# The hidden tile of the first MoE stays in PSUM until its gates

## The chip, the cores and the metric

The kernel runs on one core of a Trainium2 chip. The core has a matrix engine (TensorE, here PE, with its weight loads as PEld), a vector engine (VectorE, DVE), a scalar engine (ScalarE, ACT), a general engine (GpSimd, POOL) and a queue engine (SyncE, SP). Each works through its own list of instructions in order and waits on semaphores for the others. Matmuls write PSUM, eight banks of 128 partitions by 512 fp32 words; everything else lies in SBUF. The metric is the device time of one launch in microseconds. The kernel before took 3349.0 us, the median of three runs (3348.02 to 3355.43).

## The reference

Three stages follow each other: a two-dimensional Fourier transform of 8 x 3072 x 256 numbers of which the real part is kept, a dense MoE layer with 2048 hidden units, and a routed MoE with 8 experts of 1024 hidden units, where each token goes to one expert.

```python
X = np.fft.fft(np.fft.fft(x, axis=1), axis=2).real          # 8 x 3072 x 256
h = X.reshape(-1, 256) @ w_in                               # 24576 x 2048
g = h * np.clip(h + 3.0, 0.0, 6.0) / 6.0
y = g @ w_out                                               # 24576 x 256
logits = y @ w_gate                                         # 8 experts
e = argmax(logits); p = softmax(logits)[e]
out = p * (np.maximum(y @ w1[e], 0.0) @ w2[e])              # by expert
```

## The kernel before, in words

Precision comes from pairs: a number is kept as a rounded high part and the rest as a low part, and a product takes three matmuls (high-high, high-low, low-high).

The first phase runs the Fourier transform and the first MoE. The transform along the 256 columns is folded into `w_in`, which gives the two stacks `WA` and `WB`; the transform along the 3072 rows is done by pieces: folds of the input (`fold_quarter`, `fold_whole`, mostly on VectorE, part on GpSimd), splits into high and low (`stack_splits`), and matmuls against tables (`fft_g0`, `fft_g12`). There are 24 groups (8 batches by 3), each of two chunks of 256 column pairs, that is 512 tokens. A chunk takes 8 steps, one for each 256 hidden units, so that phase one has 384 steps; 48 of them make a batch.

`step(s)` (L943) records one step: `mm1` makes the tile `ab` (14 matmuls of 256 columns into two banks, one for WA and one for WB); `mm2` of the step three back adds its gated tile `gh`, `gl` to the four accumulators `acc` (24 matmuls of 264 columns); then come the vector parts. `h_of` (L493) copies the first bank to `A` on ScalarE (L496), and VectorE writes A minus the second bank and A plus the second bank to the two halves of `h` in SBUF (L184 and L181 are the helpers `sub` and `add`). For the step before, `relu6` (L501, ScalarE) makes `r` from `h`, `gate_h` (L508, VectorE) writes min(r, 1) times h over `r`, ScalarE rounds it to `gh` (L959), and GpSimd writes the rest `gl` (L184). So `r`, `gh` and `gl` of step s carry the number s + 1 in the names before.

PSUM: the pool `ab_ps` has two tiles of two banks, `acc` takes the other four banks. Every piece of the row transform takes a tile of `ab_ps` too (`f`, `fe`, `fo`), and so do the preparations of the weights in the first ten steps (`wi`, `wot`) and a few parts near the end (`exa`, `exo`, `ec`, `rk`). A tile is free when all that read it are done.

Every eighth step (s % 8 = 2) ends a chunk: the accumulators are copied out (`xo`, L532), cut into halves (`xp`, L539, two instructions), the tokens are routed (`rt_...` on VectorE, counts and scattered rows by GpSimd), and one piece of the next transform runs in the same step, six in a batch.

The order on each engine is set by a scheduler that lists instructions by priority and by a forecast of when their inputs are ready; `keep_in_program_order` pins an instruction to the order in which it was recorded. In the kernel before it pins the folds on VectorE (`pinned`), not the matmuls. The second phase, the routed MoE (from about 2150 us on), is not touched.

Of the kernel before, what the change touches and what calls it, by code (L numbers as in the profile page):

```python
# [10 lines left out]
F32 = mybir.dt.float32  # L11
# [5 lines left out]
AF = mybir.ActivationFunctionType  # L17
# [9 lines left out]
GW = 264  # L27
# [16 lines left out]
EC = 5  # L44
EX = 6
RKW = 4
BUFS = dict(h=2, r=4, gh=4, gl=4)
EXTRA = 23
LATE = (0, 0, 1, 1, 2, 3, 3, 4, 5, 5, 6, 6, 7, 7, 8, 8, 8, 9)
RK = 2  # L50
# [24 lines left out]
def tile_fft_moe(ctx, tc, xr, xf, xcoef, w_in, w_out, w_gate, w1, w2, tabs, fm, misc, tri, sgn8, dstc, maskc, out):  # L75
# [24 lines left out]
    tiles, hold = {}, {}  # L100
# [21 lines left out]
    def wo(i, f):  # L122
        if (i, f // 8) not in WOh:
            WOh[i, f // 8] = pc.tile([P, 8, GW], F32R, tag=f"WO{i}{f // 8}", name=f"WO{i}{f // 8}")
        return WOh[i, f // 8][:, f % 8]
# [20 lines left out]
    dve, act, pool, pe, sp = nc.vector, nc.scalar, nc.gpsimd, nc.tensor, nc.sync  # L146
# [6 lines left out]
    def ab_tile(name):  # L153
        hold["last"] = t = ab_ps.tile([P, 2, 512], F32, tag="ab", name=name)
        return t


    def bank(name):
        if "hp" in hold:
            return hold["hp"].tile([P, 512], F32, tag="hp", name=name)  # L160
        return ab_tile(name)[:, 1]

    def mm_group(dst, terms):
        for n, (l, r) in enumerate(terms):
            pe.matmul(dst, l, r, start=(n == 0), stop=(n == len(terms) - 1))  # L165

    def pinned(i):
        if hold.get("fold"):
# [11 lines left out]
    def add(eng, o, a, b):  # L180
        pinned(eng.tensor_tensor(out=o, in0=a, in1=b, op=ALU.add))  # L181

    def sub(eng, o, a, b):
        i = eng.tensor_tensor(out=o, in0=a, in1=b, op=ALU.subtract)  # L184
        pinned(i)
        return i
# [82 lines left out]
    def fft_g0(b, pq):  # L269
        def e_mm(st):  # L270
            ab = st["ab"] = ab_tile(f"fe{b}_0")
            mm_group(ab[:, 0, 0:258], fft_terms(SC0, 0, 0, "c", 0) + xterm(b, X_T0, 258))
            mm_group(ab[:, 1, 0:256], fft_terms(SC0, 1, 0, "c", 1))

        def e_ev(st):
            ab = st["ab"]
            v = lambda i: pq[:, i].rearrange("p (a c) -> p a c", a=2)
            act.activation(v(0), ab[:, :, 0:256], AF.Copy)
            dve.tensor_copy(pex[:, b:b + 1], ab[:, 0, 256:257])
            dve.tensor_tensor(out=v(1), in0=ab[:, :, 0:256], in1=v(0), op=ALU.subtract)  # L280

        def o_mm(st):
            ab = st["ab2"] = ab_tile(f"fo{b}_0")
            for i, n, c0 in ((0, 258, X_T0 + P), (1, 256, X_T1)):
                full = fft_terms(SS0, 1 - i, 0, "s", i) + xterm(b, c0, n)
                edge = fft_terms(SC0, i, P, "c", i, 1)
                for t, (l, r) in enumerate(full[:1] + edge + full[1:]):
                    rows = slice(0, 1 if 0 < t <= len(edge) else P)
                    pe.matmul(ab[rows, i, 0:n], l, r, start=t == 0, stop=t == len(full + edge) - 1)

        def o_ev(st):
            ab = st["ab2"]
            v = lambda i: pq[:, i].rearrange("p (a c) -> p a c", a=2)
            act.activation(v(2), ab[:, :, 0:256], AF.Copy)
            dve.tensor_copy(qex[:, b:b + 1], ab[:, 0, 256:257])
            dve.tensor_tensor(out=v(3), in0=ab[:, :, 0:256], in1=v(2), op=ALU.subtract)

        return [(e_mm, e_ev), (o_mm, o_ev)]
# [191 lines left out]
        for i in range(2):  # L490
            mm_group(ab[:, 1, i * 256:(i + 1) * 256], [(WB[a][:, f[i]], pq[:, 2 + c, c0:c0 + 256]) for a, c in PASS])

    def h_of(ab, h, s):  # L493
        A = pw.tile([P, 2, 256], F32, tag="Ac", bufs=AB, name=f"A{s}")
        v = [ab[:, n].rearrange("p (i n) -> p i n", i=2) for n in range(2)]
        act.activation(A, v[0], AF.Copy)  # L496
        sub(dve, h[0], A, v[1])
        add(dve, h[1], A, v[1])

    def relu6(r, h):  # L500
        act.activation(r, h, AF.Relu, bias=half, scale=1.0 / 6.0)  # L501


    def halves(tag, dt, s):
        return [pw.tile([P, 2, 256], dt, tag=tag, bufs=BUFS[tag], name=f"{tag}{s}_{n}") for n in range(2)]

    def gate_h(g, r, h):
        dve.scalar_tensor_tensor(out=g, in0=r, scalar=1.0, in1=h, op0=ALU.min, op1=ALU.mult)  # L508

    def mm2(acc, gh, gl, f0, first, last, mid=(), ntau=4):  # L510
        def one(i, t, g, w, st, sp_):
            lhs = g[t // 2][:, i, (t % 2) * P:(t % 2 + 1) * P]
            pe.matmul(acc[t][:, 0:GW], lhs, wo(w, f0 + i), start=st, stop=sp_)  # L513
        for i in range(2):
            for t in range(ntau):
                one(i, t, gh, 0, first and i == 0, False)
                one(i, t, gh, 1, False, False)
            if i == 0:
                for f in mid:
                    f()  # L520
        if last:
            for t in range(ntau):
                for i in range(2):
                    one(i, t, gl, 0, False, i == 1)
        else:
            for i in range(2):
                for t in range(ntau):
                    one(i, t, gl, 0, False, False)
# [78 lines left out]
    if True:  # L607
# [52 lines left out]
        NS = len(chunks) * STEPS  # L660
# [257 lines left out]
        def plan_early():  # L918
            e0 = 8 * (NCH - EC) + 18 + RKW - 3
            fill[e0].append(lambda: None)  # L920
            pfill[e0].append(early_mm)
            fill[e0].append(early_pick)
            fill[e0 + 4].append(lambda: (first_sets(), load_x(0), load_w(0), load_x(1)))
            for n in range(4):
                fill[e0 + 6 + EG * n].append(lambda n=n: in_order(prep_w(0, lambda n: dve)[n]))
            fill[e0 + 10 + EX].append(lambda: prep_x(0))

        def step(s):
            z = s - LAG
            if s < NS:  # L930
                b, g, c = chunks[s // STEPS]
                f0 = 2 * (s % STEPS)
                ab = ab_tile(f"ab{s}")
                mm1(ab, f0, gt[(b, g)], c * 256, q3[s // STEPS % 2])
            hold["ride"] = None
            for f in pfill.pop(s, []):
                f()
            hold["ride"] = None
            if 0 <= z < NS:
                k = z % STEPS  # L940
                if k == 0:
                    hold["acc"] = [ac_ps.tile([P, 512], F32, tag=f"acc{t}", name=f"acc{z}_{t}") for t in range(4)]
                mm2(hold["acc"], *hold.pop(("g", z)), 2 * k, k == 0, k == STEPS - 1, mfill.pop(s, []))  # L943
            for f in afill.pop(s, []):
                f()
            hold["ride"] = None
            if s < NS:
                h = hold["h", s] = halves("h", F32, s)
                h_of(ab, h, s)
            if 0 < s <= NS:  # L950
                h = hold.pop(("h", s - 1))
                r, gh, gl = halves("r", F32, s), halves("gh", F32R, s), halves("gl", F32R, s)
                g = r
                for n in range(2):
                    relu6(r[n], h[n])
                for n in range(2):
                    gate_h(g[n], r[n], h[n])
                for n in range(2):
                    act.activation(gh[n], g[n], AF.Copy)  # L959
                for n in range(2):  # L960
                    sub(pool, gl[n], g[n], gh[n])
                hold[("g", s - 1)] = (gh, gl)
            if 0 <= z < NS and z % STEPS == STEPS - 1:
                xo = pw.tile([P, 4, GW], F32, tag="xo", bufs=1, name=f"xo{z}")
                xp = pw.tile([P, 4, XW], I32, tag="xp", name=f"xp{z}")
                with tc.high_priority(offset=6):
                    evac(hold["acc"], xo)
                halve(xo, xp)
                ci = z // STEPS
                b, g, c = chunks[ci]  # L970
                plan_routing(routing(xo, xp, ci * 4, 4, 0 if (g == 0 and c == 0) else None, f"c{ci}",
                             RKW if ci < NCH - 2 else 3), s + 1)
            for f in fill.pop(s, []):
                f()
            if s % STEPS == QB and s + STEPS < NS:
                load_q3(s // STEPS + 1)

        x0 = (NB - 1) * 6 * STEPS + EXTRA
        fill[x0 - 1].append(lambda: plan_extra(x0))
        plan_early()  # L980
        for s in range(NS + LAG):
            step(s)
        ps1.close()
        h_ps = ctx.enter_context(tc.tile_pool(name="h_ps", bufs=4, space=PSUM, reuse_waits="tile"))
        o_ps = ctx.enter_context(tc.tile_pool(name="o_ps", bufs=4, space=PSUM, reuse_waits="tile"))
# [33 lines left out]
        ge = pw.tile([P, NTILE, NE + 1], F32, tag="xp", name="ge")  # L1019
        tt = pw.tile([P, NTILE, NE], F32, tag="r", bufs=BUFS["r"], name="tt")  # L1020
        dve.memset(ge[:, :, 0:1], 1.0)
# [94 lines left out]
        full = last  # L1116
# [3 lines left out]
        n = nc.values_load(nus[0:1, 0:1], min_val=0, max_val=NSMALL, skip_runtime_bounds_check_because=why)  # L1120
# [159 lines left out]
```

## Time and profile before

| | |
|---|---|
| median of three runs | 3349.0 us |
| the profiled execution | 3351.21 us, span 3349.4 us |
| mean granted TensorE clock | 0.979 |
| PE busy | 3133.1 us (94%) |
| PEld busy | 3001.7 us (90%) |
| DVE busy | 2277.1 us (68%) |
| ACT busy | 1934.1 us (58%) |
| POOL busy | 2267.7 us (68%) |

The profile is of one execution. Busy shares are means over the two phases; matmul ends are modelled, so that a busy PE isn't yet PE at its peak. The chain that ended last is 45% PE, 18% DVE, 17% ACT and 9% issue. A wait is put down to what ended it last.

### The profile page before, as it was taken

The numbers are of one execution on the slowest core, as the hardware profiler recorded it, in microseconds if no ns is written. First come the engines' busy times: TensorE is split into PE (matmuls) and PEld (weight loads), VectorE is DVE, ScalarE is ACT, GpSimd is POOL, SyncE is SP. The second block draws the span as 40 slices with busy tenths as digits, with TensorE's granted clock in tenths as the row PEclk, the third lists the DMA queues.
The fourth block names the chain that finished last, engine by engine and source line by source line (L and its number), as shares of the span: only waits on it lengthen the run. The fifth ranks groups of instructions, "written<-read, shape, count | busy, mean of one in ns | idle before, by whom it ended". The sixth has DMA issues, their size and how long they took to land.

```text
span 3349.4 us, 62616 instructions
## 1 busy us (share of the span) xinstructions
PE 3133.1 (94%) x23482; PEld 3001.7 (90%) x23482; DVE 2277.1 (68%) x3699; ACT 1934.1 (58%) x3339; POOL 2267.7 (68%) x1784
## 2 busy tenths in 40 slices
PE   5899999999999999999899999999999999999998
PEld 5899999899899899899899999988888888898887
DVE  8878777777777777777777676755555555555553
ACT  3566666566666566666566666645454444544453
POOL 5567776776776777677777776766676666666664
PEclk8999999999999999999999999999999999999999
DMA  5100100100100110000000002065555555545560
GB/s 180 61 28 21 36 25 14 43 24 16 39 28 16 33 33 16 30 30 17 31 14 16 14 18 51 20 193 154 144 168 149 143 149 158 147 145 154 147 171 30
DMA packets 256195, 243.18 MB, mean 73 GB/s; under 512 B 157739, under 2 KB 219020, under 8 KB 255888
## 3 DMA queue, kind: packets, MB, share of 16 engines
q1 hardware_dynamic: 234640, 184.66, 19.7%
q0 software_dynamic: 21248, 54.48, 4.5%
q8 instruction: 187, 3.06, 0.4%
q14 instruction: 120, 0.98, 0.1%
HBM read 159.71 MB, written 54.04 MB: 64 GB/s over the span
## 4 chain that ended last, share of the span: by engine, by line
PE 45%; DVE 18%; ACT 17%; issue 9%; POOL 5%; SPq 0%; DMA 0%; ACTq 0%; POOLq 0%; DVEq 0%
PE op L165 16%; PE hp L165 15%; PE acc L513 8%; ACT gh L959 7%; ACT r L501 6%; PE ab L165 5%; DVE h L184 4%; POOL gl L184 3%; DVE r L508 2%; POOL xs_dram L149 2%; DVE R L189 2%; DVE R L181 2%; DVE H L181 1%; ACT xp L539 1%; ACT xo L532 1%
## 5 line engine op out<-in xcount | busy, mean ns | idle before, releaser
L184 POOL TENSOR_TENSOR gl<-r,gh 128x512 fp32r<-128x512 f32 x768 | 1109.6, 1464 | 468.1 <-ACT gh L959 372.7
L501 ACT ACTIVATE r<-h,half 128x512 f32<-128x512 f32 x768 | 546.4, 719 | 610.1 <-DVE h L184 386.0
L508 DVE SCALAR_TENSOR_TENSOR r<-r,h 128x512 f32<-128x512 f32 x768 | 625.1, 818 | 369.3 <-ACT r L501 368.2
L513 PE MATMUL acc<-WO,gh 128*128 128x264 f32 x6144 | 824.4, 287 | 3.4 <-ACT xo L532 3.4
L513 PEld LDWEIGHTS acc<-WO,gh 128*128 128x128 f32 x6144 | 786.2, 192 | 3.6 <-ACT xo L532 3.6
L165 PE MATMUL ab<-pq,WA 128*128 128x256 f32 x2304 | 398.8, 290 | 107.4 <-DVE h L181 68.4
L995 DVE SCALAR_TENSOR_TENSOR WB<-hp,WA 128x512 fp32r<-128x512 f32 (+1 forms) x472 | 278.5, 606 | 301.8 <-ACT WA L994 301.7
L959 ACT ACTIVATE gh<-r 128x512 fp32r<-128x512 f32 x768 | 451.1, 622 | 42.6 <-DVE r L508 13.6
L513 PE MATMUL acc<-WO,gl 128*128 128x264 f32 x3072 | 444.6, 286 | 2.7 <-POOL gl L184 1.8
L165 PEld LDWEIGHTS ab<-pq,WA 128*128 128x128 f32 x2304 | 333.6, 193 | 120.3 <-issue 87.3
L513 PEld LDWEIGHTS acc<-WO,gl 128*128 128x128 f32 x3072 | 404.6, 189 | 6.1 <-POOL gl L184 5.6
L994 ACT ACTIVATE WA<-hp 128x512 fp32r<-128x512 f32 (+1 forms) x472 | 240.9, 529 | 197.5 <-PE hp L165 194.3
L165 PE MATMUL ab<-pq,WB 128*128 128x256 f32 x2304 | 349.2, 289 | 0.0
L149 POOL DMA_INDIRECT out_dram<-yo,dst x200 | 217.3, 1086 | 155.9 <-DVE yo L1095 118.3
L165 PEld LDWEIGHTS ab<-pq,WB 128*128 128x128 f32 x2304 | 314.2, 197 | 0.0
L149 POOL DMA_INDIRECT xs_dram<-xp,pic x192 | 212.6, 1107 | 125.6 <-DVE pic L599 68.9
L165 PE MATMUL hp<-xTb,TB 128*128 128x512 f32 (+1 forms) x1344 | 277.8, 364 | 13.9 <-DVE WB L995 13.9
L165 PE MATMUL hp<-xTa,W1b 128*128 128x512 f32 (+1 forms) x1392 | 277.0, 358 | 2.2 <-DVE WB L995 2.2
L165 PEld LDWEIGHTS hp<-xTb,TB 128*128 128x128 f32 x1344 | 226.3, 188 | 58.1 <-DVE WB L995 15.5
L165 PE MATMUL op<-W2b,WA 128*128 128x256 f32 x1536 | 276.3, 282 | 0.0
L165 PEld LDWEIGHTS hp<-xTa,W1b 128*128 128x128 f32 x1392 | 228.8, 189 | 43.3 <-DVE WB L995 2.6
L184 DVE TENSOR_TENSOR h<-A,ab 128x512 f32<-128x512 f32 x384 | 259.4, 675 | 6.7 <-ACT A L496 6.1
(269 smaller groups left out, 5479.7 us busy)
## 6 DMA issues: line engine op xcount, KB each, us to landing
w1a<-in_w_dram SPq DMA_DIRECT2D x29, 1024.0 KB
w1b<-in_w_dram SPq DMA_DIRECT2D x29, 1024.0 KB
w2b<-in_w_dram SPq DMA_DIRECT2D x58, 512.0 KB
R<-in_xr_dram SPq DMA_DIRECT2D x32, 774.0 KB
w2a<-in_w_dram SPq DMA_DIRECT2D x29, 768.0 KB
w2d<-in_w_dram SPq DMA_DIRECT2D x28, 256.0 KB
q<-pq SPq DMA_DIRECT2D x288, 1.0 KB
raw<-in_w_in_dram SPq DMA_DIRECT2D x8, 512.0 KB
```

The costliest lines, as they stand in the source:

```text
L149: i = pool.indirect_dma_start(oob_is_err=False, **kw)
L165: pe.matmul(dst, l, r, start=(n == 0), stop=(n == len(terms) - 1))
L181: pinned(eng.tensor_tensor(out=o, in0=a, in1=b, op=ALU.add))
L184: i = eng.tensor_tensor(out=o, in0=a, in1=b, op=ALU.subtract)
L189: pinned(dve.scalar_tensor_tensor(out=o, in0=a, scalar=s, in1=b, op0=ALU.mult, op1=ALU.add))
L501: act.activation(r, h, AF.Relu, bias=half, scale=1.0 / 6.0)
L508: dve.scalar_tensor_tensor(out=g, in0=r, scalar=1.0, in1=h, op0=ALU.min, op1=ALU.mult)
L513: pe.matmul(acc[t][:, 0:GW], lhs, wo(w, f0 + i), start=st, stop=sp_)
L532: act.activation(xo[:, t, :], acc[t][:, 0:GW], AF.Copy)
L959: act.activation(gh[n], g[n], AF.Copy)
L994: act.activation(hi, ps, AF.Relu)
L995: dve.scalar_tensor_tensor(out=lo, in0=ps, scalar=0.0, in1=hi, op0=ALU.max, op1=ALU.subtract)
```

## The change

`h` has no place in SBUF any more. `h_of` writes the difference and the sum over the two banks of the `ab` tile they were made from, and `relu6` and `gate_h` read them there; a tile of `ab_ps` is free only after both gates. ReLU is recorded in the step that makes h, the gates, the rounding and the rest one step later. While the steps are recorded (`hold["steps"]`), each matmul of the helpers is pinned to the program's order. `gl` has six buffers in place of four, and `h` none.

```diff
-BUFS = dict(h=2, r=4, gh=4, gl=4)
+BUFS = dict(r=4, gh=4, gl=6)
...
+    def matmul(*a, **kw):
+        i = pe.matmul(*a, **kw)
+        if hold.get("steps"):
+            tc.keep_in_program_order(i)
+
     def mm_group(dst, terms):
         for n, (l, r) in enumerate(terms):
-            pe.matmul(dst, l, r, start=(n == 0), stop=(n == len(terms) - 1))
+            matmul(dst, l, r, start=(n == 0), stop=(n == len(terms) - 1))
...
-    def h_of(ab, h, s):
+    def h_of(ab, s):
         A = pw.tile([P, 2, 256], F32, tag="Ac", bufs=AB, name=f"A{s}")
-        v = [ab[:, n].rearrange("p (i n) -> p i n", i=2) for n in range(2)]
-        act.activation(A, v[0], AF.Copy)
-        sub(dve, h[0], A, v[1])
-        add(dve, h[1], A, v[1])
+        h = [ab[:, n].rearrange("p (i n) -> p i n", i=2) for n in range(2)]
+        act.activation(A, h[0], AF.Copy)
+        sub(dve, h[0], A, h[1])
+        add(dve, h[1], A, h[1])
+        return h
...
             if s < NS:
-                h = hold["h", s] = halves("h", F32, s)
-                h_of(ab, h, s)
-            if 0 < s <= NS:
-                h = hold.pop(("h", s - 1))
+                h = h_of(ab, s)
                 r, gh, gl = halves("r", F32, s), halves("gh", F32R, s), halves("gl", F32R, s)
-                g = r
                 for n in range(2):
                     relu6(r[n], h[n])
+                hold["r", s] = h, r, gh, gl
+            if 0 < s <= NS:
+                h, r, gh, gl = hold.pop(("r", s - 1))
                 for n in range(2):
-                    gate_h(g[n], r[n], h[n])
+                    gate_h(r[n], r[n], h[n])
...
+        hold["steps"] = True
         for s in range(NS + LAG):
             step(s)
+        hold["steps"] = False
```

The second matmul loops of `fft_g0` and `mm2` call the same helper. Three places show what the order becomes.

ScalarE at the end of a chunk, step 106, before. `r107` is made from the h of step 106, `xo103` and `xp103` are the chunk's result, `vc2` is the transform's second bank:

```order
L496 ACTIVATE A106_8267<-ab106_8210 128x512
L501 ACTIVATE r107_0_8360<-h106_0_8265,half_101 128x512
L959 ACTIVATE gh106_0_8273<-r106_0_8271 128x512
L532 ACTIVATE xo103_8285<-acc96_0_7759 128x264
L532 ACTIVATE xo103_8285<-acc96_1_7760 128x264
L532 ACTIVATE xo103_8285<-acc96_2_7761 128x264
L959 ACTIVATE gh106_1_8274<-r106_1_8272 128x512
L532 ACTIVATE xo103_8285<-acc96_3_7762 128x264
L501 ACTIVATE r107_1_8361<-h106_1_8266,half_101 128x512
L539 ACTIVATE xp103_8286<-xo103_8285 128x4x256 x2
L321 ACTIVATE vc2_1_1_8293<-f2_1_1_8249 128x258
L496 ACTIVATE A107_8356<-ab107_8311 128x512
```

The same place now (names carry the step's own number):

```order
L502 ACTIVATE A106_8061<-ab106_8006 128x512
L965 ACTIVATE gh105_0_7993<-r105_0_7991 128x512
L965 ACTIVATE gh105_1_7994<-r105_1_7992 128x512
L508 ACTIVATE r106_0_8065<-ab106_8006,half_101 128x512
L508 ACTIVATE r106_1_8066<-ab106_8006,half_101 128x512
L539 ACTIVATE xo103_8079<-acc96_0_7569 128x264
L539 ACTIVATE xo103_8079<-acc96_1_7570 128x264
L539 ACTIVATE xo103_8079<-acc96_2_7571 128x264
L539 ACTIVATE xo103_8079<-acc96_3_7572 128x264
L326 ACTIVATE vc2_1_1_8087<-f2_1_1_8045 128x258
L546 ACTIVATE xp103_8080<-xo103_8079 128x4x256 x2
L182 ACTIVATE pq2_1_7493<-pf2_1_1_8088 128x512
```

The two roundings `gh` stand ahead of the two `r`, and no longer between them, and `vc` stands ahead of `xp`. In a plain step the list is A, r, gh, gh, r before and A, gh, gh, r, r now.

VectorE in plain steps, 109 and the start of 110, before; L189 is a fold of the transform's input:

```order
L184 TENSOR_TENSOR h109_0_8493<-A109_8495,ab109_8454 128x512
L181 TENSOR_TENSOR h109_1_8494<-A109_8495,ab109_8454 128x512
L508 SCALAR_TENSOR_TENSOR r110_0_8574<-r110_0_8574,h109_0_8493 128x512
L508 SCALAR_TENSOR_TENSOR r110_1_8575<-r110_1_8575,h109_1_8494 128x512
L189 SCALAR_TENSOR_TENSOR R3_1_1_8087<-R3_1_1_8087 128x6x129
L184 TENSOR_TENSOR h110_0_8568<-A110_8570,ab110_8529 128x512
```

The same steps now:

```order
L189 TENSOR_TENSOR ab109_8244<-A109_8283,ab109_8244 128x512
L186 TENSOR_TENSOR R3_1_1_7887<-R3_1_1_7887 128x6x129
L186 TENSOR_TENSOR ab109_8244<-A109_8283,ab109_8244 128x512
L515 SCALAR_TENSOR_TENSOR r109_0_8287<-r109_0_8287,ab109_8244 128x512
L515 SCALAR_TENSOR_TENSOR r109_1_8288<-r109_1_8288,ab109_8244 128x512
L189 TENSOR_TENSOR ab110_8317<-A110_8356,ab110_8317 128x512
L194 SCALAR_TENSOR_TENSOR R3_1_1_7887<-R3_1_1_7887 128x6x129
```

The fold moved from behind the gates to between the difference and the sum. The gates of a step stand ahead of the next step's h in both lists, though they are recorded behind it now.

TensorE in the first steps, behind `mm1` of step 3, before; `wot` and `wi` prepare weights:

```order
L513 MATMUL acc0_3_677<-WO10_491,gh1_1_479 128x264
L513 MATMUL acc0_0_674<-WO00_490,gl1_0_480 128x264
L473 MATMUL wot1_634<-ident_95,rawo_148 128x128 x4
L513 MATMUL acc0_1_675<-WO00_490,gl1_0_480 128x264
L513 MATMUL acc0_2_676<-WO00_490,gl1_1_481 128x264
L513 MATMUL acc0_3_677<-WO00_490,gl1_1_481 128x264
L513 MATMUL acc0_0_674<-WO00_490,gl1_0_480 128x264
L513 MATMUL acc0_1_675<-WO00_490,gl1_0_480 128x264
L513 MATMUL acc0_2_676<-WO00_490,gl1_1_481 128x264
L513 MATMUL acc0_3_677<-WO00_490,gl1_1_481 128x264
L165 MATMUL wi5_645<-SC1_74,fmt_140 128x256 x4
L165 MATMUL wot1_634<-wg_158,wotT1_639 128x8 x4
```

The same place now:

```order
L164 MATMUL ab3_621<-pq0_0_213,WB1_72 128x256
L478 MATMUL wot1_636<-ident_95,rawo_148 128x128 x4
L164 MATMUL wot1_636<-wg_158,wotT1_641 128x8 x4
L164 MATMUL wi5_647<-SC1_74,fmt_140 128x256 x12
L164 MATMUL wi5_647<-fmt_140,SC1_74 128x2 x4
L164 MATMUL wi5_647<-SC1_74,fmt_140 128x128 x4
L164 MATMUL wi5_647<-fmt_140,SC1_74 128x2 x4
L164 MATMUL wi5_647<-SC1_74,fmt_140 128x128 x4
L164 MATMUL acc0_0_676<-WO00_494,gh0_0_407 128x264
```

`wot` and `wi` stood in and behind the accumulator's matmuls, and stand ahead of them now, right behind `mm1`. From step 13 to step 361 the matmuls stand in the same order in both.

## Rows read from the trace of the kernel before

**Rows 1.** Busy time by window: us, busy us (count) by engine, clock, DMA share, GB/s.

```profile
868.00:1127.00 259.00, 239.91 (x1925) 235.90 (x1925) 198.44 (x329) 164.53 (x305) 184.96 (x167) 0.98 0.08 26
```

**Rows 2.** TensorE's waits, 1055 to 1314.6 us: total us, times, longest.

```profile
PE ab L165 <- DVE h L181: 10.1, 7, 2.0
...
PE acc L513 <- POOL gl L184: 0.2, 1, 0.2
```

**Rows 3.** Timeline of TensorE: start us, us, instruction, count, idle time before it.

```profile
1013.96 0.86 PE L165 MATMUL f<-TB,SC 128*128 128x256 f32 x6
...
1015.68 0.59 PE L165 MATMUL ab<-pq,WA 128*128 128x256 f32 x3
...
1040.11 0.52 PE L165 MATMUL ab<-pq,WA 128*128 128x256 f32 x3
...
1044.67 0.52 PE L165 MATMUL ab<-pq,WA 128*128 128x256 f32 x3
...
1055.03 0.95 PE L165 MATMUL fe<-TB,SC0s 128*128 128x258 f32 x6 [0.78 <-DVE h L181]
...
1058.89 0.59 PE L165 MATMUL ab<-pq,WA 128*128 128x256 f32 x3 [2.01 <-DVE h L181]
...
1314.60 0.95 PE L165 MATMUL fe<-TB,SC0s 128*128 128x258 f32 x6 [0.78 <-DVE h L181]
```

**Rows 4.** Busy time by window, just behind the wait of 2.01 us.

```profile
1060.00:1063.80 3.80, 3.80 (x21) 3.80 (x21) 2.18 (x5) 3.80 (x8) 2.25 (x3) 0.58 0.01 2
```

**Rows 5.** Timeline of VectorE, two steps with a fold ahead of them.

```profile
1051.91 1.78 DVE L189 SCALAR_TENSOR_TENSOR H<-H 128x516 f32<-128x516 f32 x1
1053.62 0.67 DVE L184 TENSOR_TENSOR h<-A,ab 128x512 f32<-128x512 f32 x1
1054.21 0.68 DVE L181 TENSOR_TENSOR h<-A,ab 128x512 f32<-128x512 f32 x1
...
1056.80 0.75 DVE L508 SCALAR_TENSOR_TENSOR r<-r,h 128x512 f32<-128x512 f32 x1 [0.97 <-ACT r L501]
1057.47 0.67 DVE L184 TENSOR_TENSOR h<-A,ab 128x512 f32<-128x512 f32 x1
```

**Rows 6.** Timeline of ScalarE in the same steps.

```profile
1054.38 0.72 ACT L501 ACTIVATE r<-h,half 128x512 f32<-128x512 f32 x1
...
1056.06 0.71 ACT L501 ACTIVATE r<-h,half 128x512 f32<-128x512 f32 x1
```

**Rows 7.** Groups, 1055 to 1314.6 us: count | busy us, mean ns | idle before.

```profile
L508 DVE SCALAR_TENSOR_TENSOR r<-r,h 128x512 f32<-128x512 f32 x96 | 75.6, 791 | 48.3 <-ACT r L501 48.2
L184 DVE TENSOR_TENSOR h<-A,ab 128x512 f32<-128x512 f32 x48 | 32.4, 675 | 0.0
...
L189 DVE SCALAR_TENSOR_TENSOR R<-R 128x774 f32<-128x774 f32 x4 | 6.0, 1501 | 0.0
...
L181 DVE TENSOR_TENSOR R<-R 128x516 f32<-128x516 f32 x4 | 4.9, 1230 | 0.0
...
L184 POOL TENSOR_TENSOR gl<-r,gh 128x512 fp32r<-128x512 f32 x96 | 137.9, 1456 | 54.2 <-ACT gh L959 46.7 <-PE acc L513 6.4 <-DVE pf L323 0.2
L149 POOL DMA_INDIRECT xs_dram<-xp,pic x24 | 26.7, 1114 | 16.3 <-DVE pic L599 9.9 <-issue 4.6 <-DVE rt_kc L559 0.9
...
L501 ACT ACTIVATE r<-h,half 128x512 f32<-128x512 f32 x97 | 69.1, 719 | 83.7 <-DVE h L184 51.6 <-POOL gl L184 23.4 <-DVE h L181 7.0
```

**Rows 8.** A ReLU out of PSUM in the second phase, group over the span.

```profile
L994 ACT ACTIVATE WA<-hp 128x512 fp32r<-128x512 f32 x328 | 192.9, 593 | 184.0 <-PE hp L165 180.9 <-PE rkc L165 2.3 <-PE cps L1013 0.8
```

**Rows 9.** Timeline at a chunk's end: ScalarE, then TensorE.

```profile
1018.40 2.02 ACT L539 ACTIVATE xp<-xo 128x1024 uint16<-128x1024 uint16 x2
...
1021.71 0.60 PE L165 MATMUL ab<-pq,WA 128*128 128x256 f32 x3 [1.20 <-DVE rt_kc L585]
```

**Rows 10.** Timeline of TensorE, steps 3 and 4.

```profile
80.78 0.95 PE L165 MATMUL ab<-pq,WA 128*128 128x256 f32 x3
...
91.37 0.57 PE L165 MATMUL ab<-pq,WA 128*128 128x256 f32 x3
```

More of the change, by code (lines that the diff above doesn't have):

```diff
@@ L288, in o_mm @@
                     rows = slice(0, 1 if 0 < t <= len(edge) else P)
-                    pe.matmul(ab[rows, i, 0:n], l, r, start=t == 0, stop=t == len(full + edge) - 1)
+                    matmul(ab[rows, i, 0:n], l, r, start=t == 0, stop=t == len(full + edge) - 1)
         def o_ev(st):
@@ L512, in one @@
             lhs = g[t // 2][:, i, (t % 2) * P:(t % 2 + 1) * P]
-            pe.matmul(acc[t][:, 0:GW], lhs, wo(w, f0 + i), start=st, stop=sp_)
+            matmul(acc[t][:, 0:GW], lhs, wo(w, f0 + i), start=st, stop=sp_)
         for i in range(2):
@@ L947, in step @@
             if s < NS:
-                h = hold["h", s] = halves("h", F32, s)
-                h_of(ab, h, s)
-            if 0 < s <= NS:
-                h = hold.pop(("h", s - 1))
+                h = h_of(ab, s)
                 r, gh, gl = halves("r", F32, s), halves("gh", F32R, s), halves("gl", F32R, s)
-                g = r
                 for n in range(2):
                     relu6(r[n], h[n])
+                hold["r", s] = h, r, gh, gl
+            if 0 < s <= NS:
+                h, r, gh, gl = hold.pop(("r", s - 1))
                 for n in range(2):
-                    gate_h(g[n], r[n], h[n])
+                    gate_h(r[n], r[n], h[n])
                 for n in range(2):
-                    act.activation(gh[n], g[n], AF.Copy)
+                    act.activation(gh[n], r[n], AF.Copy)
                 for n in range(2):
-                    sub(pool, gl[n], g[n], gh[n])
-                hold[("g", s - 1)] = (gh, gl)
+                    sub(pool, gl[n], r[n], gh[n])
+                hold["g", s - 1] = gh, gl
             if 0 <= z < NS and z % STEPS == STEPS - 1:
```

## The prediction

> **What bounds the kernel now.** I read the busy time by window first. In one batch of the middle PE is busy 239.9 of 259 us and no other engine more than 198.4 [rows 1], so the time is PE's, and what can be gained is what PE loses. From a `fe` to the same piece one batch later takes 259.57 us, a plain step 4.56, a transform piece 1.72 [rows 3]. 48 plain steps are 218.9; five pieces at 1.72 and the longer `fo` (26 matmuls), which I take at 3.5, add 12.1: 231. So 28.5 us of a batch are lost, 4.75 at each of its six chunk ends.
>
> The waits of PE come next: seven rows, 10.1 us for VectorE's sum `h` in the first, 19.8 in all [rows 2]. They stand at the transform pieces, which take a tile of `ab_ps`: 0.78 ahead of `fe`, 2.01 ahead of the `ab` behind it [rows 3]. Behind the 2.01 the granted clock falls to 0.58 for 3.8 us [rows 4], which costs 3.8 x 0.42 = 1.6; six such are 9.6, about the rest of the 28.5.
>
> Why is `h` late? The timelines of VectorE and ScalarE show a loop. From one difference to the next lie 3.85 us without a fold; the second gate waits 0.97 in it for its `r` [rows 5], since the two roundings stand between the two `r` on ScalarE and `r1` comes only 1.68 behind `r0` [rows 6]. A fold stands behind the gates and comes on top. A long fold is 1.23 to 1.50 by group, six groups of four [rows 7]; their mean is 1.36. Of 48 steps I count 24 with a long fold, 16 with a short one (half a long one, 0.68, my estimate) and 8 without: mean loop 3.85 + (24 x 1.36 + 16 x 0.68)/48 = 4.76. The chunk end is VectorE's lump: 198.4 less 96 halves of h at 0.60, 96 gates at 0.67 (starts in a row, [rows 5]), 24 x 1.29 and 16 x 0.68 of folds leaves 34.7, or 5.8 for each of six. The chain then needs 8 x 4.76 + 5.8 = 43.9 us for a chunk; measured are 259.57/6 = 43.3. So the loop of VectorE and ScalarE sets the pace, PE (231/6 = 38.5) only waits in places where it runs out of tiles.
>
> **The loop afterwards.** The list of ScalarE becomes A, gh, gh, r, r; the fold goes between difference and sum, where it covers the first `r`. From a difference to the next: difference 0.59, fold 1.36, sum 0.68, to ScalarE 0.09, `r1` 0.71, back 0.03, second gate 0.67 [rows 5, 6] = 4.13. Without fold the second `r` follows the first: 0.67 + 0.09 + 0.68 + 0.71 + 0.03 + 0.67 = 2.85; with a short fold 3.53. Mean 3.72, so 8 x 3.72 + 5.8 = 35.6 us for a chunk, 2.9 under PE's 38.5. PE becomes the bound. The lump alone still delays things locally, up to 5.8 less the slack of the steps behind it.
>
> **Unknown prices.** No row shows VectorE writing PSUM. `h`, with one operand there, is 675 ns, the gates, with both in SBUF, 791 [rows 7]. One bound is that h written there and the gates reading it cost nothing more, with the gates down to 675 (0.23 us less per step); the other is that each of four operations takes 0.12 us more, the distance of those two rows, or 0.46 per step. I take 0, nearest to the 675. ScalarE's ReLU out of PSUM is 593 against 719 out of SBUF [rows 7, 8]: 0.12 less, in the loop; I leave it as a reserve. Even with 0.46 more the loop gives 8 x 4.18 + 5.8 = 39.2, just over PE's 38.5.
>
> The Trainium skill, Perfetto Trace Analysis, section Optimizing Scalar/DVE Operations, gives VectorE about 125 ns of access in PSUM against 60 in SBUF; by that my estimate would be 4 x 0.065 = 0.26 more per step, a chunk of 37.7, 0.8 under PE's instead of 2.9. It speaks against the change; the row with 675 beside 791 doesn't show it.
>
> The same skill, SBUF — State Buffer, section SBUF: two separate sides, says that a VectorE instruction with two SBUF inputs locks the port it shares with GpSimd, where that reads SBUF too. Gates with one input in PSUM would be free of it: by my estimate 675, and the time some 29 us below my forecast. The trace agrees that the operation with one PSUM operand is shorter, 675 against 791, not that the lock is why.
>
> **The bank is held longer.** Its tile came free at the end of the sum, 1054.21 + 0.68; now at the end of the second gate, 1056.80 + 0.75 by the old order [rows 5]: 2.66 later. A tile is now released some 5.5 us after its `mm1` began: 14 matmuls at 1.72/12 [rows 3], 2.0; the copy A at 0.59, as another ScalarE operation out of PSUM [rows 8]; the loop's 2.85. In a plain step `ab` two steps on wants it after 2 x 4.56 = 9.1, so there it is covered. At a piece, which takes the other tile, the next `ab` wants it after 4.56 + 1.72 = 6.3 [rows 3], and a sixth to a quarter of the lump, 0.9 to 1.4, moves the release to 6.4 to 6.9. So 0.1 to 0.6 of wait per chunk stays. The lump of GpSimd stays too: four scatters of 1.1 with their counts hold `gl` up [rows 7], ScalarE's `r` waited 23.4 us for `gl` in a batch; six buffers help there, but `mm2` needs `gl` all the same: about 1.35 per chunk (0.8 as a wait of `ab`, 0.55 as a wait for `gl`), and 0.4 for chunks with heavy splits. The 1.20 that `ab` waited for `rt_kc`, behind a `xp` of 2.02 on ScalarE [rows 9], goes, as `vc` now stands ahead of `xp`. Left: 2.2 of the 4.75 per chunk, waits too short to pull the clock down. Gain 2.55 x 36 chunk ends (batches 1 to 6) = 92.
>
> **The ends of the phase.** Batch 0 has five more chunk ends; I take half of the gain, -6. In the first steps pinned `wot` and `wi` go right behind `mm1` and need the other tile, now held for the gates, where `mm2` matmuls stood between. PE waits 1.5 to 3 us there in four steps, but a step of that stretch takes 10.6 us anyway [rows 10], so part is hidden: 0 to +15, taken +8. The same for `exa`, `exo`, `ec`, `rk` near the end: +4. Sum: 3351.2 - 92 - 6 + 8 + 4 = 3265 against the profiled execution's 3351.2, which is 2 above the median; so 3262.
>
> **The rivals.**
> - *Everything vanishes.* With the loop 2.9 under PE no chunk end loses anything: 36 x 4.75 = 171 and batch 0's 6 gained, the ends' 12 lost, 2 for the median: 3184. For it: the shorter `r` and perhaps shorter gates. Against: the GpSimd lump, which isn't touched. 0.14.
> - *Partial.* PSUM prices or the held bank make the loop 0.2 to 0.46 longer; the chunk lands between 38.5 and 41.5 with its residual, gain 15 to 55: 3295 to 3335. For it: bounds above. 0.14.
> - *No change.* The held bank takes back what the order gives, as `r` of the step then waits for a sum that stands behind a fold: 3349. Needs a residual of 4.75, twice my estimate. 0.06.
> - *Slower.* The bank's hold decides: if the loop's mean stays at 4.69 or more ((43.3 - 5.8)/8, one us over my sum), the chain is as late as before, and each of 36 chunk ends waits up to 2.66 longer: 36 x 1.33 to 36 x 2.66 = 48 to 96, about 3420. The Trainium skill, Perfetto Trace Analysis, section Optimization Strategy, says that a bubble that repeats can mean too few tiles in PSUM: this change keeps the tiles longer, and by that rule the repeated waits of PE grow. The rows agree that PE waits for tiles, but put what is late on VectorE's chain. 0.14.
>
> **How the numbers follow.** Forecast 0.52, its own range 3225 to 3310 (residual 1.2 to 3.7 per chunk). From what a measurement of this kernel can tell, 0.2% or 6.7 us is no change. Faster 0.52 + 0.14 + 0.14 = 0.80; same 0.06; slower 0.14. The range leaves out the slower case and the far end of the first: 3185 to 3345.
>
> **What would show it.** The gates' idle time for `r` (48.3 a batch) should fall under 15, ScalarE's `r` wait for h and `gl` (83.7) [rows 7] should now mostly be room; `fe` to `fe` should be near 244; the granted clock stays near 1.00 behind pieces; PE's waits are for gates and `gl`, none near 2 us. The prediction is wrong if `ab` still waits 2 us behind pieces, now for the second gate; if difference to difference with a fold stays over 4.6; if halves written to PSUM take over 800 ns; or if steps 2 to 10 lose more than 15 us.

## The result and the profile after

The changed kernel took 3305.16 us, the median of four runs (3300.97 to 3309.74), against 3349.8 (median of four) of the kernel before on the same chip: a ratio of 0.9868, 95% interval 0.9854 to 0.9881, or 40 to 49 us less. The forecast was 3262. The direction is the forecast's, the gain is half of it.

The two profiled executions, cut at the first matmul of a batch's first `mm1` (us; the changed kernel's profile is of the run of 3300.97):

| part | before | after | difference | forecast |
|---|---|---|---|---|
| to step 0 | 45.9 | 46.3 | +0.4 | |
| batch 0 | 304.4 | 319.4 | +15.0 | +2 |
| batches 1 to 6 | 1553.1 | 1490.0 | -63.2 | -92 |
| batch 7, to its last step | 244.5 | 249.2 | +4.8 | +4 |
| the rest | 1201.5 | 1194.0 | -7.5 | 0 |

The rest is the second phase, which the change doesn't touch; it took 1195 to 1200 us in the profiles of the other kernels below, whether or not they have the change, so I take its 7.5 for a difference between single executions. Batches 1 to 6 gave two thirds of what was forecast, and batch 0 took back 15.

TensorE in one batch of the changed kernel, columns as in [rows 1]:

```profile
1040.50:1288.60 248.10, 236.07 (x1933) 233.38 (x1932) 175.83 (x332) 169.58 (x306) 168.52 (x167) 0.99 0.09 28
```

VectorE is busy 175.8 us where it was 198.4, and the batch is 11 us shorter. What TensorE waited for in it (total, times, longest), to be set beside [rows 2]:

```profile
PE ab L164 <- DVE r L515: 9.0, 10, 2.2
PE f L164 <- DVE r L515: 1.4, 1, 1.4
PE fe L164 <- DVE r L515: 0.9, 2, 0.5
PE ab L164 <- DVE rt_mc L558: 0.8, 1, 0.8
```

12.1 us are left of 19.8, and the tile is now released by the gates (L515). The forecast said that no wait near 2 us would be left. TensorE's timeline at the place of [rows 3], and one `fe` two batches on:

```profile
1041.65 0.96 PE L164 MATMUL fe<-TB,SC0s 128*128 128x258 f32 x6 [0.55 <-DVE r L515]
...
1045.67 0.59 PE L164 MATMUL ab<-pq,WA 128*128 128x256 f32 x3 [2.17 <-DVE r L515]
...
1540.36 0.96 PE L164 MATMUL fe<-TB,SC0s 128*128 128x258 f32 x6 [0.55 <-DVE r L515]
```

Two batches take 498.7, 249.4 each, not the forecast's 244. The wait behind `fe` is still there, 2.17 where it was 2.01. Behind this one the granted clock holds (window as in [rows 4]):

```profile
1046.80:1050.60 3.80, 3.80 (x34) 3.80 (x33) 2.95 (x15) 2.86 (x6) 2.12 (x3) 1.00 0.13 39
```

Not behind every one: 125 us on, in the same batch, `ab` waits 2.15 (to 1170.65) and the clock is 0.55 from 1171.3 to 1175.1. The kernel before has both cases too. In its batch of [rows 2] the clock falls behind three of four such waits, and behind the fourth, 2.02 us long to 1235.01, it stays at 1.00. So a wait of 2 us does not in itself bring the clock down. VectorE in a step without a fold, to be set beside [rows 5]:

```profile
1063.08 0.69 DVE L189 TENSOR_TENSOR ab<-A,ab 128x512 f32<-128x512 f32 x1
1063.81 0.70 DVE L186 TENSOR_TENSOR ab<-A,ab 128x512 f32<-128x512 f32 x1
1065.89 1.28 DVE L515 SCALAR_TENSOR_TENSOR r<-r,ab 128x512 f32<-128x512 f32 x2 [1.39 <-ACT r L508]
1067.10 0.69 DVE L189 TENSOR_TENSOR ab<-A,ab 128x512 f32<-128x512 f32 x1
```

and ScalarE in that step, to be set beside [rows 6]:

```profile
1064.60 1.27 ACT L508 ACTIVATE r<-ab,half 128x512 f32<-128x512 f32 x2 [0.68 <-DVE ab L186]
```

From difference to difference are 4.02 us, more than the 3.85 of before and far from the 2.85 of the forecast. The first ReLU starts 0.09 behind the end of the sum, not of the difference; the first gate starts when both ReLU are done, and VectorE stands idle 1.39 us between the sum and the gates. A step with a fold between the two:

```profile
1108.51 0.69 DVE L189 TENSOR_TENSOR ab<-A,ab 128x512 f32<-128x512 f32 x1
1109.10 1.76 DVE L186 TENSOR_TENSOR R<-R 128x516 f32<-128x516 f32 x1
1110.79 0.68 DVE L186 TENSOR_TENSOR ab<-A,ab 128x512 f32<-128x512 f32 x1
1112.87 1.29 DVE L515 SCALAR_TENSOR_TENSOR r<-r,ab 128x512 f32<-128x512 f32 x2 [1.40 <-ACT r L508]
1114.07 0.69 DVE L189 TENSOR_TENSOR ab<-A,ab 128x512 f32<-128x512 f32 x1
```

It takes 5.56, the 4.02 and all but 0.22 of the fold. Groups of the batch, as in [rows 7]:

```profile
L515 DVE SCALAR_TENSOR_TENSOR r<-r,ab 128x512 f32<-128x512 f32 x98 | 63.0, 685 | 67.6 <-ACT r L508 66.3 <-issue 1.2
L189 DVE TENSOR_TENSOR ab<-A,ab 128x512 f32<-128x512 f32 x49 | 33.8, 690 | 2.8 <-issue 1.5 <-ACT A L502 1.1
...
L186 DVE TENSOR_TENSOR R<-R 128x516 f32<-128x516 f32 x4 | 5.2, 1308 | 0.0
...
L186 DVE TENSOR_TENSOR R<-R 128x774 f32<-128x774 f32 x4 | 4.7, 1168 | 0.0
L194 DVE SCALAR_TENSOR_TENSOR R<-R 128x774 f32<-128x774 f32 x4 | 4.2, 1061 | 0.0
...
L186 DVE TENSOR_TENSOR H<-H 128x516 f32<-128x516 f32 x4 | 2.8, 690 | 0.0
...
L508 ACT ACTIVATE r<-ab,half 128x512 f32<-128x512 f32 x96 | 61.0, 683 | 34.2 <-DVE ab L186 29.2 <-POOL gl L189 2.7 <-POOL cnt L581 2.3
```

The gates' idle time for `r` rose from 48.3 to 66.3 us, where under 15 was forecast. But the gates take 685 ns and not 791, writing h to PSUM costs 690 against 675, and the 24 long folds average 1.06 us (mean of the six groups) against 1.36. The loop got longer, and the work in and between its turns got shorter by more.

### The profile page after: what moved, and what is told of

The parts are those of the page before. It is cut to its first block, busy times and chain, and to the rows that moved or that the text cites. A ratio compares the mean times of both kernels' runs of the same rounds, so it can differ in the third digit from the quotient of the medians.

```text
span 3298.9 us, 61794 instructions
## 1 busy us (share of the span) xinstructions
PE 3107.9 (94%) x23482; PEld 2982.5 (90%) x23482; DVE 2092.7 (63%) x3699; ACT 1955.3 (59%) x3339; POOL 2116.0 (64%) x1784
## 5 line engine op out<-in xcount | busy, mean ns | idle before, releaser
L189 POOL TENSOR_TENSOR gl<-r,gh 128x512 fp32r<-128x512 f32 x768 | 1012.5, 1341 | 511.1 <-ACT gh L965 479.2
L515 DVE SCALAR_TENSOR_TENSOR r<-r,ab 128x512 f32<-128x512 f32 x768 | 494.5, 684 | 513.6 <-ACT r L508 506.3
L508 ACT ACTIVATE r<-ab,half 128x512 f32<-128x512 f32 x768 | 485.6, 682 | 229.0 <-DVE ab L186 201.6
L164 PE MATMUL ab<-pq,WB 128*128 128x256 f32 x2304 | 341.3, 284 | 0.0
L502 ACT ACTIVATE A<-ab 128x512 f32<-128x512 f32 x384 | 230.4, 600 | 146.1 <-PE ab L164 129.3
L164 PEld LDWEIGHTS ab<-pq,WB 128*128 128x128 f32 x2304 | 306.5, 192 | 0.0
L189 DVE TENSOR_TENSOR ab<-A,ab 128x512 f32<-128x512 f32 x384 | 265.3, 691 | 48.7 <-ACT A L502 39.0
L149 POOL DMA_INDIRECT xs_dram<-xp,pic x192 | 192.6, 1003 | 140.6 <-DVE rt_kc L566 56.2
```

The lines of the kernel that those rows point to most:

```text
L149: i = pool.indirect_dma_start(oob_is_err=False, **kw)
L164: i = pe.matmul(*a, **kw)
L502: act.activation(A, h[0], AF.Copy)
```

## The experiments

Two theories. **Theory 1:** the forecast's loop failed because of two waits that the trace of before could not show, the first ReLU on the sum and the first gate on the second ReLU; they ate the missing gain. **Theory 2:** what gain there is comes from VectorE's instructions with two SBUF inputs, which run less beside GpSimd's `gl`. All are against the kernel before, whose runs had medians of 3348.9 to 3351.4 in the three sets. The loop is VectorE's, difference to difference without a fold. With the second wait away 3.44 is its length where VectorE does not wait for the next A; more than half of its turns do wait, and last 4.1 to 4.7. The batch is the mean of batches 1 to 6.

| run | median us | ratio, 95% interval | loop | gates ns | batch |
|---|---|---|---|---|---|
| before | 3349.8 | | 3.85 | 818 | 258.9 |
| changed | 3305.2 | 0.9868 (0.9854 to 0.9881) | 4.02 | 684 | 248.3 |
| both waits away | 3210.1 | 0.9587 (0.9574 to 0.9600) | 3.60 | 686 | 234.9 |
| first wait away | 3295.7 | 0.9832 (0.9816 to 0.9848) | 3.80 | 683 | 248.0 |
| second wait away | 3204.4 | 0.9567 (0.9549 to 0.9585) | 3.44 | 684 | 234.3 |
| changed, h in SBUF | 3392.6 | 1.0133 (1.0117 to 1.0148) | 3.86 | 961 | 265.3 |
| before, gl zeros | 3148.4 | one run | | 698 | 231.1 |
| changed, gl zeros | 3216.8 | one run | | 684 | 236.2 |

The gates' ns are means over the whole span here.

**Both waits away.** The halves of a tile lie in two banks, so neither wait guards anything; each is declared as no dependency:

```diff
+                rr = [relu6(r[n], h[n]) for n in range(2)]
+                tc.declare_no_dep(rr[0].ins, hold["add"].ins.name, reason="two banks")
...
+                gg = [gate_h(r[n], r[n], h[n]) for n in range(2)]
+                tc.declare_no_dep(gg[0].ins, rr[1].ins.name, reason="two banks")
```

> The changed kernel, but the two halves of an ab tile no longer wait for each other: the first ReLU waits for the difference alone (in the changed kernel it starts 0.10 us behind the sum in every step), the first gate for the first ReLU alone. The list of ScalarE becomes A, r, gh, r, gh again, and the folds stand behind the gates as before. Theory 1, these waits ate the gain that was forecast: the loop without a fold falls from 4.02 to about 3.6 us and the time to 3265 to 3285. Theory 2, the gain came from VectorE's instructions with two SBUF inputs running less beside GpSimd's gl: folds behind the gates fall beside gl again (a 774-element fold back from 1.1 to 1.5 us), and the time is 3310 to 3340, though the gates stay at 685 ns.

It came to 3210, below both theories' numbers. VectorE in a step without a fold:

```profile
1068.53 0.68 DVE L191 TENSOR_TENSOR ab<-A,ab 128x512 f32<-128x512 f32 x1
1069.25 0.70 DVE L186 TENSOR_TENSOR ab<-A,ab 128x512 f32<-128x512 f32 x1
1070.03 0.69 DVE L517 SCALAR_TENSOR_TENSOR r<-r,ab 128x512 f32<-128x512 f32 x1
1071.13 0.69 DVE L517 SCALAR_TENSOR_TENSOR r<-r,ab 128x512 f32<-128x512 f32 x1 [0.41 <-ACT r L510]
1072.13 0.70 DVE L191 TENSOR_TENSOR ab<-A,ab 128x512 f32<-128x512 f32 x1 [0.32 <-ACT A L504]
```

The loop is 3.60 as theory 1 said, and at its end VectorE already waits for A, the copy of the next step: TensorE is the bound there. The batch is 234.9, near the 231 of pure matmuls. The 774-element folds did go back up, to 1.24 and 1.32 us over the span, the part of theory 2 that held; the mean of all long folds in batches 1 to 6 stayed (1.08, 1.07 in the changed kernel). I had turned the loop into too little time. Once the chain passes below TensorE's step the waits at the pieces go as well: TensorE waits 2.8 us for tiles in 235 us, where it waited 12.1 in a batch of the changed kernel.

**One wait at a time**, the one or the other of the two lines above.

> Of the two waits taken away in the run that came to 3210 us, only the first: the first ReLU waits for the difference alone, the first gate still for both ReLU. ScalarE keeps the changed kernel's list A, gh, gh, r, r; the folds go behind the gates. If each wait costs about one instruction of the loop (0.6 us of the 4.02 without a fold), the loop falls to 3.4 and the time to 3225 to 3265. Rival: the second wait alone holds the loop, and this run stays within 15 us of 3305.

> Only the second wait taken away: the first gate follows the first ReLU, which still waits for the sum. ScalarE's list as in the changed kernel, folds behind the gates. By the same reckoning a loop of 3.4 and 3225 to 3265. Rival: the first wait alone holds the loop, within 15 us of 3305.

The first alone gave 3296, its rival's case; the second alone 3204, more than expected. VectorE with the second wait away:

```profile
1064.12 0.69 DVE L191 TENSOR_TENSOR ab<-A,ab 128x512 f32<-128x512 f32 x1
1064.85 0.70 DVE L186 TENSOR_TENSOR ab<-A,ab 128x512 f32<-128x512 f32 x1
1066.36 1.28 DVE L517 SCALAR_TENSOR_TENSOR r<-r,ab 128x512 f32<-128x512 f32 x2 [0.81 <-ACT r L510]
1067.56 0.69 DVE L191 TENSOR_TENSOR ab<-A,ab 128x512 f32<-128x512 f32 x1
```

The idle time ahead of the gates falls from 1.39 to 0.81, one ReLU (0.58), and the loop to 3.44. With the first wait away the first ReLU does come earlier, but a rounding then slips in between the two ReLU, and both gates wait for the second all the same:

```profile
1061.54 0.69 DVE L191 TENSOR_TENSOR ab<-A,ab 128x512 f32<-128x512 f32 x1
1062.26 0.69 DVE L186 TENSOR_TENSOR ab<-A,ab 128x512 f32<-128x512 f32 x1
1064.14 1.29 DVE L517 SCALAR_TENSOR_TENSOR r<-r,ab 128x512 f32<-128x512 f32 x2 [1.18 <-ACT r L510]
```

ScalarE in that step:

```profile
1062.32 0.69 ACT L510 ACTIVATE r<-ab,half 128x512 f32<-128x512 f32 x1 [1.01 <-DVE ab L191]
1062.90 0.62 ACT L966 ACTIVATE gh<-r 128x512 fp32r<-128x512 f32 x1
1063.42 0.68 ACT L510 ACTIVATE r<-ab,half 128x512 f32<-128x512 f32 x1
```

So the list of ScalarE was not the A, gh, gh, r, r that I had expected. The loop does fall there, from 4.02 to 3.80, but the batch stays at 248: the folds now stand behind the gates, where nothing hides them, and take 1.37 on the mean. They stand there with the second wait away too, so their place is not what gains the time. The wait that matters is the first gate's for the second ReLU.

**h in SBUF, the rest as changed.** `h_of` writes to two tiles of SBUF (`gl` with four buffers, for the space).

```diff
-        h = [ab[:, n].rearrange("p (i n) -> p i n", i=2) for n in range(2)]
+        v = [ab[:, n].rearrange("p (i n) -> p i n", i=2) for n in range(2)]
...
-                h = h_of(ab, s)
+                h = h_of(ab, halves("h", F32, s), s)
```

> The changed kernel with h in SBUF again (two buffers, gl with four for the space): recording order and TensorE's order as changed. Theory 2 (place of h): gates go back to about 790 ns, the time to 3335 to 3360. Theory 1 (waits and order): h by halves lets the first ReLU follow the difference, and TensorE's order is that of the change, so the time is 3290 to 3310 or less.

3393, slower than before and than either theory had it. It has neither of the two waits and the same list of ScalarE (A, r, gh, r, gh) as the run with both away. So 182 us lie between the two, with h in PSUM or not (and two buffers of `gl`, below). The main reason stands in the second gate, here of the run with h in SBUF, VectorE:

```profile
1061.38 0.69 DVE L515 SCALAR_TENSOR_TENSOR r<-r,h 128x512 f32<-128x512 f32 x1 [0.25 <-ACT r L508]
1062.52 1.27 DVE L515 SCALAR_TENSOR_TENSOR r<-r,h 128x512 f32<-128x512 f32 x1 [0.44 <-ACT r L508]
```

and GpSimd beside it:

```profile
1061.95 2.98 POOL L189 TENSOR_TENSOR gl<-r,gh 128x512 fp32r<-128x512 f32 x2 [2.29 <-ACT gh L965]
```

The second gate starts 0.57 into `gl` and takes 1.27. With h in PSUM and both waits away, `gl` starts in the same way ahead of the second gate, and the gate takes 0.69. VectorE and GpSimd of that run:

```profile
1063.19 0.69 DVE L517 SCALAR_TENSOR_TENSOR r<-r,ab 128x512 f32<-128x512 f32 x1 [0.41 <-ACT r L510]
```

```profile
1062.65 3.01 POOL L191 TENSOR_TENSOR gl<-r,gh 128x512 fp32r<-128x512 f32 x2 [0.83 <-ACT gh L967]
```

Over a batch the gates make 0.275 x 96 = 26 us of difference, and the long folds 8 more (1.42 on the mean with h in SBUF, 1.08 with h in PSUM); the batches differ by 30.

**GpSimd reads nothing.** In the kernel before and in the changed one, `gl` is filled with zeros.

```diff
-                    sub(pool, gl[n], g[n], gh[n])
+                    pool.memset(gl[n].bitcast(F32), 0.0)
```

> The kernel before, with gl filled with zeros by GpSimd in place of r minus gh (the low part of the gated tile is left out): GpSimd then reads nothing from SBUF in these 768 instructions. If VectorE's instructions with two SBUF inputs are lengthened by GpSimd's reads, the gates fall from 791 to under 700 ns and the long folds from 1.23 to 1.50 us to 0.7 to 1.1. Rival: their length is their own or ScalarE's doing: gates at 770 to 800, folds as before. The time falls in either case if GpSimd's gl was waited for (some 15 to 60 us), so the time does not decide, the durations do.

> The changed kernel with gl filled with zeros by GpSimd (the low part of the gated tile is left out), so that GpSimd reads nothing in these instructions. By the chain's sum: loop without a fold 4.02 as in the changed kernel, folds at 1.0 and 0.7 us in place of 1.06 on the mean, 8 x 4.5 + 4.7 = 40.7 us for a chunk, 244 for a batch in place of 248.3, 3270 to 3285 in all; gates stay at 680 to 690, since they have one operand in SBUF. Rival: what is left in the changed kernel is GpSimd's gl itself, and the batch falls to 231 as it did with the same replacement in the kernel before (3148), 3180 to 3200.

In the kernel before, with h in SBUF as ever, groups of 1040.5 to 1288.6 us:

```profile
L508 DVE SCALAR_TENSOR_TENSOR r<-r,h 128x512 f32<-128x512 f32 x104 | 72.7, 703 | 42.5 <-ACT r L501 42.2
...
L189 DVE SCALAR_TENSOR_TENSOR R<-R 128x774 f32<-128x774 f32 x4 | 4.3, 1070 | 0.0
L181 DVE TENSOR_TENSOR R<-R 128x774 f32<-128x774 f32 x4 | 3.8, 958 | 0.0
```

Gates of 791 fall to 703 and folds of 1.50 to about 1.0 with VectorE's program unchanged. GpSimd is also busy for a shorter time there, but the traces tell the two apart. In batches 1 to 6 of the kernel before the 75 long folds that begin while a `gl` runs take 2.05 us (774 elements) or 1.78 (516); the other 63 take 0.96 or 0.69, also the 12 of them into which a `gl` begins. With zeros, 12 folds begin while GpSimd writes `gl`, and take 0.96 or 0.69. So GpSimd writing does not lengthen them; GpSimd reading ahead of them does. The batch falls to 231.1, TensorE alone. The zeros are also written sooner (529 ns against 1456) and wait for no rounding, so the time of this run is no price of GpSimd's reading by itself. In the changed kernel the same replacement leaves the gates at 684 and gives 236.2 a batch. Both my numbers there missed: 244 was too slow, since a fold between difference and sum adds 0.22 less than its length (a difference to the next with a fold of 0.69 is 4.49) and the lump was put at 4.7; the rival's 231 was too fast. With the folds at 0.78 on the mean, 4.02 + (24 x 0.56 + 16 x 0.2)/48 = 4.37, and the changed kernel's lump of 4.2 (below), 39.2 for a chunk; measured 39.4. The loop of 4.02 holds this run above TensorE's 38.5.

**TensorE's order.** Pinned from step 12 on (in the changed kernel, with both waits away, and with the second away), pinned in the kernel before, and not pinned at all with the second wait away:

```diff
-        hold["steps"] = True
         for s in range(NS + LAG):
+            hold["steps"] = s >= 12
             step(s)
```

> The changed kernel, TensorE held to the program's order only from step 12 on. If the order is what costs the first steps their 15 us (batch 0 took 304.4 before and 319.4 after), batch 0 falls to 304 to 308 and the time by 10 to 15, to 3290 to 3295. Rival: the tiles held for the gates cost it, whatever the order: within 4 us of the changed kernel's 3305.

> The two waits taken away and TensorE's order pinned from step 12 on. If the two gains add up, 3198 to 3204 (10.6 less than 3210; batch 0 at 298 to 300). Rival: with the waits gone the start is hardly delayed by the order (batch 0 was 310 there, 5.6 above before), so 3205 to 3210.

> The second wait alone taken away (the run of 3204 us), TensorE's order pinned from step 12 on. With both waits away the later pin gave 12 us; if it does so here, 3190 to 3196, the shortest so far. Rival: batch 0 was 306 here against 310 there, so there is less to gain, 3198 to 3204.

> The kernel before, with TensorE alone held to the program's order from the first step. If the order costs at the start only, as the run with the pin from step 12 on showed for the changed kernel (10.6 us), the time is 3354 to 3362 with a batch in the middle as before (259.5). Rival: the order gains in the middle and is part of the change's gain, 3320 to 3343. Rival: it costs in the middle too and is why h in SBUF with the change's order came to 3393, above 3370.

> The same kernel (second wait away) without any pin on TensorE's matmuls. If the pin does nothing but order the start, as in the kernel before (3352.8 with it against 3349.8), 3190 to 3198, like the pin from step 12 on. Rival: with h in PSUM the scheduler moves matmuls of the accumulators around the transform pieces, and a batch in the middle is longer than 234: 3210 or more.

| run | median us | ratio, 95% interval | batch 0 | batch |
|---|---|---|---|---|
| changed, pinned from 12 | 3294.6 | 0.9836 (0.9822 to 0.9849) | 306.4 | 248.4 |
| both waits away, from 12 | 3197.8 | 0.9540 (0.9525 to 0.9555) | 294.8 | 235.1 |
| second away, from 12 | 3200.6 | 0.9554 (0.9541 to 0.9568) | 307.0 | 234.1 |
| before, pinned | 3352.8 | 1.0005 (0.9995 to 1.0015) | 304.2 | 260.9 |
| second away, no pin | 3188.1 | 0.9512 (0.9499 to 0.9525) | 303.7 | 233.1 |

In the changed kernel the later pin takes 10.6 us off the time, and batch 0 falls from 319.4 to 306.4. With both waits away it takes off 12. In the kernel before the pin changes nothing that can be told (batch 0 is 304.2 with it, and I had expected 4 to 12 us more), and with the second wait away the later pin gains 4, within its interval, as the rival had it. Without any pin that kernel is the shortest of all, 16 us by the medians under its pinned form; its batch in the middle is shorter too, 233.1 against 234.3. So the pin was no part of the gain. What it costs at the start hangs on the rest of the order: pinned from the first step and from step 12, batch 0 is 306.1 and 307.0 with the second wait away, 310.0 and 294.8 with both. The changed kernel itself was not run without it.

**Buffers of gl.** The kernel with the second wait away, four buffers and not six.

> The kernel of 3204 us (second wait away) with four buffers of gl in place of six; the run with h in SBUF had four as well. If gl's buffers don't matter, within 6 us of 3204, and the 3393 of h in SBUF is owed to h. Rival: ReLU waits for gl at the chunk's end (23.4 us a batch in the kernel before), 3220 to 3260.

3214.8 (ratio 0.9595, 0.9582 to 0.9608) against 0.9567: some 9 us by the medians, a little over what was expected. The executions of the two kernels overlap (3203.6 to 3216.6 here, 3200.9 to 3212.1 with six buffers), and the one in the profile is the shortest of its five, so its batch of 235.0 does not show where the 9 us lie. Of the 182 us between h in SBUF and h in PSUM it explains one in twenty.

## Why the prediction was right in direction and wrong in size

**The direction** came out right, but not by the term that was to bring it, and that is luck. The gain was to come from a shorter loop, and the loop got longer. Three runs part the change: its order with h in SBUF costs 44 us (3349 to 3393), h in PSUM takes off 182 (to 3210, some 9 of it by the buffers of `gl`), and the two waits that came with the shared tile put 95 back (to 3305).

**What bounds the kernel.** The sum 8 x (loop + folds) + lump held for other kernels than the one it was made from, once its terms were read from their own traces. For the changed one: 4.02 + (24 x 0.84 + 16 x 0.3)/48 = 4.54 with the folds' 1.06 less 0.22, and a lump (VectorE's work at a chunk's end) of 4.2 by the same subtraction, 40.5 us for a chunk; measured 248.3/6 = 41.4. It forecast the bound that would follow, TensorE's 38.5, and the runs with the second wait away stand at 234.3/6 = 39.0. One reading was wrong: the prediction counts the fall of the clock six times in a batch, 9.6 us. In its batch the clock falls three times, to 0.56 to 0.61 for 3.8 us each, which is 4.8 by the same reckoning; with the 19.8 of waits some 4 of the 28.5 us stay unexplained.

**The loop afterwards: the step that failed.** It put 2.85 without a fold: the difference, both ReLU and the second gate in a row, the sum lying beside the first ReLU and the first gate beside the second. Measured are 4.02, with all six in a row: 0.73 from difference to sum, 2.08 from the sum to the gates (the sum itself 0.70, both ReLU 1.27, the ways between), 1.21 for both gates. So the sum came onto the path with 0.70, and the gates with 0.54 more than the 0.67 of one. (The sum also no longer overlaps the difference, 0.73 behind its start and not 0.59. It writes the bank that the difference reads, which I take for the reason; no run tests it.) The two had been taken as lying beside the ReLU because in the kernel before each half of `h` was a tile of its own and waited alone. In `ab` the halves share a tile, and each half is waited for with the other, though nothing in the data asks for it. The order of the changed kernel showed that the two ReLU stand together and the two gates together; I read it as a better order and did not ask what wait had brought them together. The second of these waits, taken away alone with the lists that the scheduler then makes, is worth 101 us; the first alone is worth 10.

**The fold** that went between difference and sum was to cover the first ReLU. It does not: the first ReLU waits for the sum, which stands behind the fold, and only 0.22 of the fold is hidden. Nor did all folds go there: of 97 steps with one long fold and nothing else in batches 1 to 6, 34 still have it behind the gates. (The 3.53 put for a short fold should be 3.45 by the terms of the 4.13; that moves the mean by 0.03.)

**Unknown prices.** Writing PSUM costs 15 ns more (690 against 675), the gates fell by 106 (685), ReLU by 36 (683 against 719), not by the 126 held in reserve. Taking 0 erred on the dear side. The Trainium skill, Perfetto Trace Analysis, section Optimizing Scalar/DVE Operations, gives the figures by which the prediction estimated 0.065 more for each of four of VectorE's operations. The trace doesn't agree: it shows 0.015 more for h, and shorter gates.

**The skill's other rule**, on VectorE and GpSimd in SBUF, is what carried the gain. The second gate beside `gl` takes 1.27 us with both inputs in SBUF and 0.69 with one in PSUM; with GpSimd reading nothing, gates and folds are short in SBUF also. By the Trainium skill, SBUF — State Buffer, section SBUF: two separate sides, that is the port which a VectorE instruction with two SBUF inputs shares with a GpSimd instruction that reads SBUF. The traces agree on both conditions: one input moved to PSUM makes the gate short, and so does GpSimd writing without reading. I gave it 29 us as an aside, with no working, and left it out of the sum. That the folds, `rt_dc` (899 ns before, 225 now) and the lump shrink too, I had not seen: they have two inputs in SBUF as before, and fewer of them begin while a `gl` runs (of the long folds in batches 1 to 6 38 now, 75 before).

**The bank held longer** costs 12.1 us a batch in waits, as against 13.2 forecast, but for another reason: the gates are late by the loop, not by the hold. With the second wait away TensorE waits 3.1 us over a whole batch, at a bank held until the gates just the same. So the hold is nearly free. The slower rival, which lets the hold decide, did not come about; the loop it needed (4.69 with folds) was missed by 0.15.

**The start** was forecast at 0 to +15, taken +8, and batch 0 with its five chunk ends at +2; batch 0 is +15. Of that 10.6 lie in the first 12 steps, and all but 0.8 of them go when the pin begins at step 12; the other 4.4 lie behind them, where -6 was forecast for the chunk ends. From step 3 to step 4 TensorE takes 18.8 us in place of the 10.6 of [rows 10]:

```profile
80.36 0.57 PE L164 MATMUL ab<-pq,WA 128*128 128x256 f32 x3
...
99.19 0.67 PE L164 MATMUL ab<-pq,WA 128*128 128x256 f32 x3
```

**The rivals.** The time lies in the range of the partial one (3295 to 3335), which put it down to PSUM's price or the held bank; both are measured and neither is the cause. Of the four signs of being wrong two came: `ab` waits 2 us behind pieces for the second gate, and difference to difference with a fold is over 4.6 (5.04 on the mean where a long fold lies between). The halves written to PSUM (690 ns, not 800) and steps 2 to 10 (9 us lost, not 15) gave none.

## What to carry to other kernels

When two halves of one tile replace two tiles, look for what now waits for the whole: an engine's two instructions that have moved together in the list are the sign, and a dependency that guards nothing can be declared away. Ask of each vector instruction how many of its inputs lie in SBUF while GpSimd reads there: moving one input to PSUM was worth more here than the order of the step. A chain's period, counted from start to start with all that stands in it, told the pace of three of these kernels to within 3% once its waits were read from their own traces.

## What the runs showed of the hardware

A gate of 128x512 beside GpSimd's subtraction takes 1.27 us with both inputs in SBUF and 0.69 with one in PSUM. VectorE writes a 128x512 result to PSUM in place in 690 ns, against 675 to SBUF. A fold of two SBUF inputs that begins while GpSimd's subtraction runs takes 2.05 us for 774 elements, one that begins before it 0.96 (kernel before). The granted clock fell to 0.58 behind a wait of 2.01 us and held at 1.00 behind one of 2.02 in the kernel before; in the changed one it fell to 0.55 behind 2.15 and held behind 2.17. No run here tells what decides.
